# First MLP products by Strassen's scheme, with stored weight operands and unsplit attention

## The chip, the core and the metric

The kernel runs on one core of a Trainium2 chip. The metric is the device time of one execution in microseconds. Before the change three runs gave 1202.59, 1205.68 and 1206.07 us, median 1205.68.

## What is computed

The reference is a retention layer, then two MLPs. All tensors of activations are float32; the weights arrive as 8-byte floats. Cut to what matters:

```python
# q, k, v: (4, 8, 768, 64);  gamma = 1 - 2**(-5 - head)
for t in range(768):
    state = gamma * state + outer(k[:, :, t], v[:, :, t])
    y[:, :, t] = (1 / 8) * q[:, :, t] @ state
x = y.transpose(0, 2, 1, 3).reshape(3072, 512)
h = x @ w_in                      # (512, 2048)
x = np.maximum(0.01 * h, h) @ w_out
h = np.maximum(x @ w_in2, 0)
out = (h * h) @ w_out2            # (3072, 512)
```

## The kernel before

The sequence is cut into three chunks of 256 tokens; a pair is one chunk of one batch entry (`u` in the code) and two heads. For a pair the kernel makes scaled queries `qs` and values `vs`, the masked scores `pm`, the values product `y` and, but for the last chunk, the state that the next chunk starts from (`outer`, `sp`). Pairs with `u` under `WHOLE` (the first chunk) use full float32 matmuls. Later ones split every operand into a high part and a remainder in the `F32R` type (`kh`, `kl`, `q2`, `v2`, `ph`, `w2`) and add up partial products of these.

The MLPs run over six blocks of 512 tokens per layer and, in a block, over 16 steps, one per 128 hidden columns. A step makes the first product (`emit_in`, L407: 4 row blocks x 3 passes = 12 matmuls of 512 columns into one PSUM tile `h`), the activation (`activate`), the split of `g` into `gh` and `gl` (L431, L432), and the second product (`emit_out`, L467: 3 passes x 4 = 12 matmuls into the four `acc` tiles). A product of split operands takes three passes: high by high, remainder by high, high by remainder. Weights are turned from 8-byte to 4-byte floats once, by `cast` (L307 to L313), and stay in SBUF; their split into high part and remainder (`split_w`, L369 and L370) is made anew for every step of every block. For the first `HS` steps of the first block full float32 matmuls of 256 columns are used.

The order on each engine is set by a scheduler that runs when the kernel is built and moves instructions by its own estimate of times; on the chip each engine then runs its list in that order. SP issues the loads and the stores, in its own order. The main loop places attention pairs beside the steps by `place`; four pairs come ahead of the first step.

Names used below: a unit of TensorE's work is one matmul of 512 columns; L numbers are lines of the kernel before unless the kernel after is named.

## Time and profile before

| | |
|---|---|
| three runs | 1202.59, 1205.68, 1206.07 us |
| span of the profiled execution | 1203.3 us; no other time of that execution is given |
| mean granted TensorE clock | 0.995 of 2.4 GHz |
| DMA traffic | 68.80 MB, 57 GB/s in the mean |
| DMA of SP's queue | 67.12 MB, 16.6% of the 16 engines' span |

The profile is of one execution. A page gives busy times by engine, the chain of work that ended last, and groups of instructions by line; the trace behind it can be asked for timelines and tables of stretches. PE is TensorE, DVE VectorE, ACT ScalarE, SP the engine that issues most DMAs. Matmuls overlap and their ends are modelled, so the distance between two starts, not the duration shown, tells the rate; some matmul records can be missing. A busy time is an average over stages with different bounds.

### The profile page before, as it was taken

What the parts mean: (1) busy time and instruction counts of PE and PEld (TensorE: products, weight loads), DVE (VectorE), ACT (ScalarE), POOL (GpSimd) and SP (SyncE); (2) the same over time, 40 slices, a digit from 0 to 9 for tenths busy, and PEclk for the clock granted to TensorE, in tenths of its full rate; (3) what the DMA queues carried; (4) which work ended last, traced back from release to release, by engine and by line L of the source; (5) the groups of instructions that cost most, each with busy time, mean ns of one, the idle gap of its engine ahead of it and who ended that gap; (6) DMA issues with size and microseconds to landing.
All of it is one profiled execution on the core that took longest, in us unless ns stands there. A gap on an engine that the chain in (4) does not pass through costs nothing.

```text
span 1203.3 us, 15155 instructions
## 1 busy us (share of the span) xinstructions
PE 1180.2 (98%) x5670; PEld 976.2 (81%) x5670; DVE 862.4 (72%) x1572; ACT 692.8 (58%) x1352; POOL 0.2 (0%) x4
## 2 busy tenths in 40 slices
PE   7799999999999999999999999999999999999998
PEld 4577788888888888888888788888888888888886
DVE  5898698888889888887888964645555545545553
ACT  4775576666667667676676654544444444444443
POOL 0000000000000000000000000000000000000000
PEclk8999999999999999999999999999999999999999
DMA  9753111111111111110144300000000000000000
GB/s 338 259 205 123 54 44 44 49 44 62 44 40 36 53 36 35 51 38 18 53 149 148 114 28 1 35 1 1 36 1 1 36 1 1 35 1 1 36 1 35
DMA packets 22824, 68.80 MB, mean 57 GB/s; under 512 B 2784, under 2 KB 5088, under 8 KB 22752
## 3 DMA queue, kind: packets, MB, share of 16 engines
q1 hardware_dynamic: 22032, 67.12, 16.6%
q8 instruction: 44, 0.72, 0.2%
q10 hardware_dynamic: 720, 0.73, 0.2%
q14 instruction: 28, 0.23, 0.1%
HBM read 61.55 MB, written 6.29 MB: 56 GB/s over the span
## 4 chain that ended last, share of the span: by engine, by line
PE 89%; DMA 4%; DVE 4%; ACT 2%; issue 1%; DVEq 0%; SPq 0%; ACTq 0%
PE acc L467 40%; PE h L407 40%; DMA sg<-w 4%; PE sc L179 2%; PE y L211 2%; PE sp L246 1%; ACT w L307 1%; PE y L231 1%; DVE w L313 1%; DVE w L310 1%; PE y L205 1%; PE sc L171 1%; PE sc L170 1%; ACT sg L308 0%; DVE w L309 0%
## 5 line engine op out<-in xcount | busy, mean ns | idle before, releaser
L407 PE MATMUL h<-xh,wih 128*128 128x512 f32 (+1 forms) x768 | 298.9, 390 | 1.1 <-DVE g L422 1.1
L407 PE MATMUL h<-xh,wil 128*128 128x512 f32 (+1 forms) x768 | 297.6, 387 | 0.8 <-DVE wil L370 0.8
L407 PE MATMUL h<-xl,wih 128*128 128x512 f32 (+1 forms) x768 | 297.6, 388 | 0.0
L370 DVE TENSOR_TENSOR wol<-w,woh 128x512 fp32r<-128x512 f32 x192 | 132.5, 690 | 150.6 <-ACT woh L369 149.2
L369 ACT CAST woh<-w 128x512 fp32r<-128x512 f32 x192 | 119.5, 622 | 183.5 <-PE acc L467 182.4
L407 PEld LDWEIGHTS h<-xh,wil 128*128 128x128 f32 x768 | 144.2, 188 | 30.3 <-DVE wil L370 1.6
L407 PEld LDWEIGHTS h<-xh,wih 128*128 128x128 f32 x768 | 144.3, 188 | 29.2 <-DVE g L422 1.3
L407 PEld LDWEIGHTS h<-xl,wih 128*128 128x128 f32 x768 | 144.2, 188 | 29.0 <-DVE w L313 0.3
L431 ACT CAST gh<-g 128x512 fp32r<-128x512 f32 (+1 forms) x192 | 118.1, 615 | 38.2 <-DVE g L425 26.4
L432 DVE TENSOR_TENSOR gl<-g,gh 128x512 fp32r<-128x512 f32 (+1 forms) x192 | 130.7, 681 | 11.4 <-ACT gh L431 3.2
L370 DVE TENSOR_TENSOR wil<-w,wih 128x512 fp32r<-128x512 f32 x192 | 131.2, 684 | 0.6 <-ACT wih L369 0.2
L369 ACT CAST wih<-w 128x512 fp32r<-128x512 f32 x192 | 117.5, 613 | 4.7 <-PE h L407 4.4
L467 PE MATMUL acc<-gh,woh 128*128 128x512 f32 (+1 forms) x388 | 111.7, 396 | 0.5 <-ACT gh L431 0.5
L425 DVE SCALAR_TENSOR_TENSOR g<-h,g 128x512 f32<-128x512 f32 x96 | 66.3, 690 | 62.9 <-ACT g L424 62.8
L467 PE MATMUL acc<-gh,wol 128*128 128x512 f32 (+1 forms) x388 | 108.9, 385 | 0.0
L467 PE MATMUL acc<-woh,gh 128*128 128x512 f32 x384 | 108.5, 389 | 0.0
L467 PE MATMUL acc<-wol,gh 128*128 128x512 f32 x384 | 108.5, 389 | 0.0
L467 PE MATMUL acc<-woh,gl 128*128 128x512 f32 x384 | 107.0, 389 | 0.0
L467 PE MATMUL acc<-gl,woh 128*128 128x512 f32 (+1 forms) x388 | 103.9, 384 | 0.0
L424 ACT ACTIVATE g<-h 128x512 f32<-128x512 f32 x96 | 57.3, 597 | 77.3 <-PE h L407 73.5
L421 ACT ACTIVATE g<-h 128x512 f32<-128x512 f32 (+1 forms) x101 | 57.9, 573 | 50.1 <-PE h L407 40.5
L467 PEld LDWEIGHTS acc<-woh,gh 128*128 128x128 f32 x384 | 72.1, 188 | 15.0
(84 smaller groups left out, 1453.8 us busy)
## 6 DMA issues: line engine op xcount, KB each, us to landing
sg<-w SPq DMA_DIRECT2D x64, 512.0 KB, 3.8
r<-attn SPq DMA_DIRECT2D x32, 512.0 KB, 3.5
out<-os SPq DMA_DIRECT2D x24, 256.0 KB, 2.2
re<-first SPq DMA_DIRECT2D x9, 512.0 KB, 5.6
r<-first SPq DMA_DIRECT2D x6, 512.0 KB, 3.9
kn<-attn SPq DMA_DIRECT2D x16, 128.0 KB, 2.0
r<-first SPq DMA_DIRECT2D x2, 256.0 KB, 3.2
qt<-qtab ACTq DMA_DIRECT2D x1, 384.0 KB, 7.8
```

The lines of the kernel that those rows point to most:

```text
L170: nc.tensor.matmul(out=sc[:, 128:256], lhsT=k[a, P:2 * P], rhs=qs[a, P:2 * P], start=True, stop=True)
L179: nc.tensor.matmul(out=sc[:, o:o + C - c], lhsT=kk[:, h * C + sb * P:h * C + (sb + 1) * P], rhs=q2[h][:, c:C], start=n == 0 and sb == 0, s ...
L211: nc.tensor.matmul(out=y[:, c:C], lhsT=v2[:, sb, h].rearrange("p a e -> p (a e)"), rhs=t[:, n, o:o + C - c], start=start, stop=n == 1 and ...
L369: nc.scalar.copy(hi, src)
L370: nc.vector.tensor_tensor(out=lo, in0=src, in1=hi.bitcast(F32), op=ALU.subtract)
L407: nc.tensor.matmul(out=hp[:, :c1 - c0], lhsT=a[:, kb * P:(kb + 1) * P], rhs=b[:, c0:c1], start=kb == 0 and k == 0, stop=kb == KB - 1 and k ...
L421: nc.scalar.activation(out=g[:, :m], in_=hp[:, :m], func=AF.Copy, scale=LEAK)
L424: nc.scalar.activation(out=g[:, :m], in_=hp[:, :m], func=AF.Relu)
L425: nc.vector.scalar_tensor_tensor(out=g[:, :m], in0=hp[:, :m], scalar=0.0, in1=g[:, :m], op0=ALU.max, op1=ALU.mult)
L431: nc.scalar.copy(gh[:, :m], g[:, :m])
L432: nc.vector.tensor_tensor(out=gl[:, :m], in0=g[:, :m], in1=gh[:, :m].bitcast(F32), op=ALU.subtract)
L467: nc.tensor.matmul(out=o, lhsT=lhsT, rhs=rhs, start=start and k == 0, stop=stop and k == 2)
```

## The change

The token blocks of both MLPs become 1024 wide, three per layer. For each group `q` of 256 hidden columns, the first product of a 512 x 256 weight with a 512 x 1024 activation is taken as a product of 2 x 2 blocks and made with seven block products in place of eight (Winograd's form of Strassen's scheme). Each block product has a contraction of 256, so two row blocks x three passes = 6 matmuls of 512 columns. The sums of weight blocks are made in `make_in`, those of activation blocks in `operands`, and those of products partly in PSUM (tile `pa` carries products 1, 6, 7 and 4 in turn and is copied in between) and partly on VectorE. The second product is as before, once for the first 512 tokens beside the group (`emit_out(lay, b, 0, ...)`, a block's first half here) and once for the other 512 after all groups (`emit_out(lay, b, 1, ...)`, its second half).

The weight operands, high part and remainder, are made once per layer, in its first block or, for four groups of the second layer, in the last block of the first layer. They are stored to DRAM by POOL's queue and read back by SP for every later block, the second product's (`wo`, 1 MB per group) twice per block. Buffers: two for `wo`; one for `wa` and `wb`, the first product's operands, until the attention is done, and two after that. The first layer's output goes through DRAM (`ydr`).

Attention is unsplit in all chunks, the scores of two heads next to each other, and the carried state is a block-diagonal 128 x 128 operand `sdiag`. All 16 pairs of the first chunk come ahead of the MLPs. Scores of later chunks use the same three PSUM tiles as the products. The leaky gate is one VectorE operation on SBUF after a plain copy, where it was a scaled ScalarE copy and a maximum. The output is written in another layout and put in order when it is returned.

Over the program the order of the kernel after holds 2016 matmuls of the first products (its L322) and 2304 of the second (L394), and SP's holds 80 loads of `wo`, 36 each of `wa` and `wb`, 47 + 2 of pairs, 32 of raw weights of 1 MB, 3 of `xs` and 48 stores; POOL's has 48 stores of weight operands.

```diff
+UNIT = {7: 0, 4: 1, 2: 2, 1: 3, 5: 4, 6: 5, 3: 6}
...
+    def swap_pools():
+        early.close()
+        late["p"] = ctx.enter_context(tc.tile_pool(name="late", bufs=1))
...
+    def scores(up):
+        qs, k, vs = prep[up]
+        k0 = 2 * (ups.index(up) % 2)
+        if up[0] < B:
+            sc = [ps_acc.tile([P, 512], F32, tag=f"acc{k0 + h}", name="sc") for h in range(2)]
+        else:
+            sc = [ps_h.tile([P, 512], F32, tag="h", name="sc") for h in range(2)]
...
+                ins = nc.tensor.matmul(out=sc[h][:, cols], lhsT=k[a, kk], rhs=qs[a, qq], start=True, stop=True)
+                if n:
+                    tc.keep_in_program_order(ins)
...
+        y = ps_a.tile([P, 2, C], F32, tag="y", name="y")
+        if c:
+            nc.tensor.matmul(out=y[:, 0], lhsT=sdiag[:, b, p], rhs=qs, start=True, stop=False)
...
+    def attend(n):
+        while n_prep[0] < min(n, len(ups)):
+            up = ups[n_prep[0]]
+            n_prep[0] += 1
+            loads_to(n_prep[0])
+            prep_pair(up)
+            scores(up)
+            loads_to(n_prep[0] + 1)
+            values(up)
...
+    def in_tiles(lay, q):
+        pool = late["p"] if late and q % 2 else w_p
+        a = pool.tile([P, 2, 4, 256], F32R, tag="wa", name="wa", bufs=1)
+        c = pool.tile([P, 2, 3, 256], F32R, tag="wb", name="wb", bufs=1)
+        return a, c
...
+    def make_in(lay, q, ahead=False):
+        load_w(lay, q, 0)
+        f = w_p.tile([P, 7, 256], F32, tag="wf", name="wf", bufs=1)
+        cast(stage.pop((lay, q, 0)), f[:, 1:5].rearrange("p n c -> p (n c)"))
+        nc.vector.tensor_tensor(out=f[:, 0], in0=f[:, 3], in1=f[:, 4], op=ALU.subtract)
+        nc.vector.tensor_tensor(out=f[:, 4], in0=f[:, 4], in1=f[:, 1], op=ALU.add)
+        nc.vector.tensor_tensor(out=f[:, 5], in0=f[:, 1], in1=f[:, 0], op=ALU.subtract)
+        nc.vector.tensor_tensor(out=f[:, 6], in0=f[:, 2], in1=f[:, 5], op=ALU.subtract)
+        if ahead:
+            a = late["p"].tile([P, 2, 4, 256], F32R, tag="ea", name="ea")
+            c = late["p"].tile([P, 2, 3, 256], F32R, tag="eb", name="eb")
+        else:
+            a, c = in_tiles(lay, q)
+        for t, s in ((a, f[:, 3:7]), (c, f[:, 0:3])):
+            nc.scalar.copy(t[:, 0], s)
+            nc.vector.tensor_tensor(out=t[:, 1], in0=s, in1=t[:, 0].bitcast(F32), op=ALU.subtract)
+        nc.gpsimd.dma_start(out=wid[lay, q][:, 0:2048], in_=a.rearrange("p l n c -> p (l n c)").bitcast(F32))
+        nc.gpsimd.dma_start(out=wid[lay, q][:, 2048:3584], in_=c.rearrange("p l n c -> p (l n c)").bitcast(F32))
+        if not ahead:
+            put_in(lay, q, a, c)
+
+    def read_in(lay, q):
+        a, c = in_tiles(lay, q)
+        nc.sync.dma_start(out=a.rearrange("p l n c -> p (l n c)").bitcast(F32), in_=wid[lay, q][:, 0:2048])
+        nc.sync.dma_start(out=c.rearrange("p l n c -> p (l n c)").bitcast(F32), in_=wid[lay, q][:, 2048:3584])
+        put_in(lay, q, a, c)
+
+    def get_in(lay, b, q):
+        (make_in if b == 0 and q >= lay * NQ // 2 else read_in)(lay, q)
+
+    def make_out(lay, q):
+        load_w(lay, q, 1)
+        f = w_p.tile([P, 1024], F32, tag="wf", name="of", bufs=1)
+        cast(stage.pop((lay, q, 1)), f)
+        o = w_p.tile([P, 2, 2, 512], F32R, tag="wo", name="wo", bufs=2)
+        fv = f.rearrange("p (j c) -> p j c", j=2)
+        nc.scalar.copy(o[:, 0], fv)
+        nc.vector.tensor_tensor(out=o[:, 1], in0=fv, in1=o[:, 0].bitcast(F32), op=ALU.subtract)
+        nc.gpsimd.dma_start(out=wod[lay, q], in_=o.rearrange("p l j c -> p (l j c)").bitcast(F32))
+        wout[lay, q] = o
+
+    def read_out(lay, q):
+        o = w_p.tile([P, 2, 2, 512], F32R, tag="wo", name="wo", bufs=2)
+        nc.sync.dma_start(out=o.rearrange("p l j c -> p (l j c)").bitcast(F32), in_=wod[lay, q])
+        wout[lay, q] = o
...
+    def operands(lay, b):
+        if lay == 1:
+            xs[NB + b] = x_p.tile([P, KB, TB], F32, tag="xs", name="xs")
+            nc.sync.dma_start(out=xs[NB + b], in_=ydr[b])
+        x = xs.pop(lay * NB + b)
+        b11, b12, b21, b22 = x[:, 0:2, 0:T], x[:, 0:2, T:TB], x[:, 2:4, 0:T], x[:, 2:4, T:TB]
+        o = {}
+        tt = nc.vector.tensor_tensor
+        o[1] = split(1, b11)
+        tt(out=b11, in0=b12, in1=b11, op=ALU.subtract)
+        o[5] = split(5, b11)
+        o[3] = split(3, b22)
+        tt(out=b12, in0=b22, in1=b12, op=ALU.subtract)
+        tt(out=b22, in0=b22, in1=b11, op=ALU.subtract)
+        o[6] = split(6, b22)
+        o[7] = split(7, b12)
+        o[2] = split(2, b21)
+        tt(out=b21, in0=b21, in1=b22, op=ALU.subtract)
+        o[4] = split(4, b21)
+        xop[lay, b] = o
...
+    def product(lay, b, q, i, ps, first_mm, last_mm):
+        w, x = win[lay, q][i], xop[lay, b][i]
+        for kt in range(2):
+            c = slice(kt * P, kt * P + P)
+            for k, (l, r) in enumerate(((0, 0), (1, 0), (0, 1))):
+                nc.tensor.matmul(
+                    out=ps, lhsT=w[l][:, c], rhs=x[r][:, kt], start=first_mm and kt == 0 and k == 0,
+                    stop=last_mm and kt == 1 and k == 2, skip_group_check=True,
+                )
...
+    def act_sbuf(lay, g, on_act):
+            nc.vector.scalar_tensor_tensor(out=g, in0=g, scalar=0.01, in1=g, op0=ALU.mult, op1=ALU.max)
...
+    def emit_in(lay, b, q):
+        j0, j1 = 2 * q, 2 * q + 1
+        pa = ps_h.tile([P, T], F32, tag="h", name="pa")
+        product(lay, b, q, 1, pa, True, True)
+        c11 = g0[j0] = keep(pa, "g", 3)
+        pd = ps_h.tile([P, T], F32, tag="h", name="pd")
+        product(lay, b, q, 5, pd, True, True)
+        c22 = g1[j1] = keep(pd, f"t{j1}", 1)
+        product(lay, b, q, 6, pa, False, True)
+        c12 = g1[j0] = keep(pa, f"t{j0}", 1)
+        product(lay, b, q, 3, pd, False, True)
+        nc.vector.tensor_tensor(out=c12, in0=c12, in1=pd, op=ALU.add)
+        act_sbuf(lay, c12, True)
+        product(lay, b, q, 7, pa, False, True)
+        nc.vector.tensor_tensor(out=c22, in0=c22, in1=pa, op=ALU.add)
+        act_sbuf(lay, c22, True)
+        pb = ps_h.tile([P, T], F32, tag="h", name="pb")
+        product(lay, b, q, 2, pb, True, True)
+        nc.vector.tensor_tensor(out=c11, in0=c11, in1=pb, op=ALU.add)
+        act_sbuf(lay, c11, False)
+        product(lay, b, q, 4, pa, False, True)
+        g = g0[j1] = g_p.tile([P, T], F32, tag="g", name="g", bufs=3)
+        if lay == 0:
+            nc.scalar.copy(g, pa)
+            act_sbuf(lay, g, False)
...
-    def split_w(i, half):
...
-        nc.scalar.copy(hi, src)
-        nc.vector.tensor_tensor(out=lo, in0=src, in1=hi.bitcast(F32), op=ALU.subtract)
...
+    attend(B * NP)
+    make_in(0, 0)
+    operands(0, 0)
+    make_out(0, 0)
+
+    for lay in range(2):
+        for b in range(NB):
+            fresh = b == 0
+            nxt = (b + 1) * B * NP if lay == 0 else 0
+            start_at = n_prep[0]
+            for q in range(NQ):
+                emit_in(lay, b, q)
+                if q + 1 < NQ:
+                    get_in(lay, b, q + 1)
+                if lay == 0 and b == NB - 1 and q % 2:
+                    make_in(1, q // 2, True)
+                if lay == 0 and b + 1 < NB:
+                    per = 1 if fresh else 2
+                    attend(start_at + per * (q + 1))
+                gg = [split_g(g0.pop(j)) for j in (2 * q, 2 * q + 1)]
+                for n, j in enumerate((2 * q, 2 * q + 1)):
+                    emit_out(lay, b, 0, j, gg[n])
+                if q + 1 < NQ:
+                    (make_out if fresh else read_out)(lay, q + 1)
+                else:
+                    read_out(lay, 0)
+            evacuate(lay, b, 0)
+            last = lay == 1 and b == NB - 1
+            if not last:
+                nl, nb = (lay, b + 1) if b + 1 < NB else (1, 0)
+            for j in range(NJ):
+                gg = split_g(g1.pop(j))
+                emit_out(lay, b, 1, j, gg)
+                if j % 2 == 1 and j + 1 < NJ:
+                    read_out(lay, j // 2 + 1)
+                if lay == 0 and b + 1 < NB and j < 8:
+                    attend(min(start_at + B * NP, n_prep[0] + 1))
+                if not last and j == 9:
+                    operands(nl, nb)
+                    get_in(nl, nb, 0)
+            if not last:
+                (make_out if nb == 0 else read_out)(nl, 0)
+            evacuate(lay, b, 1)
+            if (lay, b) == (0, NB - 2):
+                swap_pools()
```

On VectorE in the first layer, one step of the kernel before in the stage with attention (`wol`, `wil` remainders of the weights, `gl` that of the activation, the others attention and the gate):

```order
L370 TENSOR_TENSOR wol<-w,woh 128x512
L189 TENSOR_TENSOR pm<-sc,mk 128x384
L422 TENSOR_TENSOR g<-g,h 128x512
L259 TENSOR_TENSOR t<-state,sp 64x64 x2
L370 TENSOR_TENSOR wil<-w,wih 128x512
L138 TENSOR_TENSOR kl<-r,kh 128x512
L260 TENSOR_SCALAR state<-t,gt 128x64
L195 TENSOR_TENSOR ph<-pm,ph 128x384
L432 TENSOR_TENSOR gl<-g,gh 128x512
```

In the kernel after, part of one group of the first block, on VectorE (`wf`, `wa`, `wb`: the next group's weights; `pd`, `pa`: PSUM tiles of products; L334 is the gate):

```order
L352 TENSOR_TENSOR g<-g,pd 128x512
L216 TENSOR_SCALAR wf<-wf 128x1024
L334 SCALAR_TENSOR_TENSOR g<-g 128x512
L355 TENSOR_TENSOR g<-g,pa 128x512
L217 SCALAR_TENSOR_TENSOR wf<-sg,wf 128x1024
L334 SCALAR_TENSOR_TENSOR g<-g 128x512
L220 ISA wf<-sg,wf 128x2048
L133 TENSOR_TENSOR pm<-sc,mk 128x384 x2
L106 TENSOR_TENSOR qs<-r,qt 128x256
L239 TENSOR_TENSOR wf<-wf 128x256
L169 SCALAR_TENSOR_TENSOR sdiag<-sp,gt,scar 64x64 x2
L334 SCALAR_TENSOR_TENSOR g<-g 128x512
```

The remainders of weights that stood in every step are gone; conversions and sums of the next group's weights stand between the sums of this group's products, in one queue.

On TensorE in the second layer, before (`h` is a first product, `acc` the second):

```order
L407 MATMUL h<-xl_9813,wih 128x512
L407 MATMUL h<-xh_9814,wih 128x512
L407 MATMUL h<-xh_9814,wil 128x512
L467 MATMUL acc<-woh,gh 128x512 x4
L467 MATMUL acc<-wol,gh 128x512 x4
L467 MATMUL acc<-woh,gl 128x512 x4
L407 MATMUL h<-xl_9815,wih 128x512
```

and after, in the second half of a block of the second layer, where the products (`pd`, `pa`) are those of the next block:

```order
L394 MATMUL acc<-gh,wo 128x512 x8
L394 MATMUL acc<-gl,wo 128x512 x4
L394 MATMUL acc<-gh,wo 128x512 x8
L394 MATMUL acc<-gl,wo 128x512 x4
L322 MATMUL pd<-xh_7397,wa 128x512 x2
L322 MATMUL pd<-xl_7398,wa 128x512
L322 MATMUL pd<-xh_7397,wa 128x512 x2
L322 MATMUL pd<-xl_7398,wa 128x512
L394 MATMUL acc<-gh,wo 128x512 x8
L394 MATMUL acc<-gl,wo 128x512 x4
```

Both kinds of product still alternate; each run of 24 `acc` matmuls uses one `wo` tile that SP has read from DRAM.

## Rows read from the trace of the kernel before

**Rows 1.** Page, first part: busy us of each engine, share, instructions.
```profile
PE 1180.2 (98%) x5670; PEld 976.2 (81%) x5670; DVE 862.4 (72%) x1572; ACT 692.8 (58%) x1352; POOL 0.2 (0%) x4
```

**Rows 2.** Table of stretches: us; busy us (instructions) by engine; PEclk, DMA share, GB/s.
```profile
0.00:30.00 30.00, 21.63 (x107) 14.79 (x107) 17.46 (x33) 13.11 (x25) 0.20 (x4) 0.83 0.91 338
30.00:61.00 31.00, 23.66 (x136) 17.67 (x136) 27.54 (x40) 23.97 (x37) 0.00 (x0) 1.00 0.73 264
...
821.00:908.00 87.00, 87.00 (x386) 72.06 (x385) 46.89 (x72) 39.75 (x68) 0.00 (x0) 1.00 0.04 13
```

**Rows 3.** Chain of waits, second layer: start us, us, what.
```profile
848.07 4.08 PE h L407 x18
...
1109.19 4.08 PE h L407 x18
```

**Rows 4.** Timeline of TensorE, two steps with one split pair: start us, us, what.
```profile
306.32 1.17 PE L467 MATMUL acc<-gh,woh 128*128 128x512 f32 x4
...
319.82 1.17 PE L467 MATMUL acc<-gh,woh 128*128 128x512 f32 x4
```

**Rows 5.** Timeline of TensorE, unsplit pairs of the first chunk and their neighbours.
```profile
47.24 1.89 PE L397 MATMUL h<-xs,w 128*128 128x256 f32 x8
49.06 0.87 PE L231 MATMUL y<-pm,vs 128*64 128x256 f32 x8
49.86 0.50 PE L170 MATMUL sc<-qs,r 64*128 64x128 f32 x4
50.19 0.61 PE L171 MATMUL sc<-qs,r 64*128 64x256 f32 x4
...
64.22 0.49 PE L170 MATMUL sc<-qs,r 64*128 64x128 f32 x2
...
65.07 0.50 PE L407 MATMUL h<-xh,wil 128*128 128x512 f32 x1
...
93.83 0.71 PE L246 MATMUL sp<-vs,r 128*128 128x128 f32 x4
94.30 1.17 PE L467 MATMUL acc<-gh,woh 128*128 128x512 f32 x4
```

**Rows 6.** Groups by line and shape: count | busy us, mean ns of one | idle before.
```profile
L370 DVE TENSOR_TENSOR wol<-w,woh 128x512 fp32r<-128x512 f32 x192 | 132.5, 690 | 150.6 <-ACT woh L369 149.2
...
L424 ACT ACTIVATE g<-h 128x512 f32<-128x512 f32 x96 | 57.3, 597 | 77.3 <-PE h L407 73.5 <-DVE gl L432 3.6
...
L189 DVE TENSOR_TENSOR pm<-sc,mk 128x384 f32<-128x384 f32 x96 | 53.0, 555 | 24.9 <-PE sc L179 17.8 <-PE sc L171 6.1
...
L310 DVE SCALAR_TENSOR_TENSOR w<-sg,w 128x1024 uint32<-128x1024 uint32 x16 | 19.5, 1221 | 0.2
...
L313 DVE CUSTOM_DVE_ANT_0 w<-sg,w 128x2048 uint16<-128x2048 uint16 x16 | 19.5, 1221 | 1.0 <-ACT w L307 0.5
...
L123 DVE TENSOR_TENSOR qs<-r,qt 128x256 f32<-128x256 f32 x39 | 16.5, 423 | 23.6 <-DMA r<-attn 23.6
...
L309 DVE TENSOR_SCALAR w<-w 128x1024 uint32<-128x1024 uint32 x16 | 11.0, 688 | 2.2 <-ACT w L307 2.2
...
L259 DVE TENSOR_TENSOR t<-state,sp 64x64 f32<-64x64 f32 x32 | 6.9, 216 | 0.3
```

**Rows 7.** Timeline of the start: VectorE's first work on loaded data.
```profile
4.84 0.42 DVE L124 TENSOR_TENSOR vs<-r,vt 128x256 f32<-128x256 f32 x1 [3.45 <-DMA r<-first]
```

**Rows 8.** DMA issues: count, KB each, median us to landing; whole span, then 0 to 30 us.
```profile
sg<-w SPq DMA_DIRECT2D x64, 512.0 KB, 3.8
...
out<-os SPq DMA_DIRECT2D x24, 256.0 KB, 2.2
...
GB/s 0 0 124 282 315 292 260 290 329 381 410 399 434 414 421 410 421 426 399 396 391 395 392 404 426 410 399 415 410 399 421 426 344 180 104 339 273 169 388 426
...
sg<-w SPq DMA_DIRECT2D x13, 512.0 KB, 6.9
```

**Rows 9.** Timeline of the end: TensorE's last matmuls.
```profile
1197.20 1.07 PE L467 MATMUL acc<-woh,gl 128*128 128x512 f32 x4
```

More of the change, by code (lines that the diff above doesn't have):

```diff
@@ L150, in prep_pair @@
-        if chunk(u):
-            s = state[:, u % B, p]
-            w2 = st_p.tile([P, 2, 2, D], F32R, tag="w2", name="w2")
+        prep[up] = (qs, t[:, C:2 * C], vs)
+    def scores(up):
[5 more added lines that the diff above has]
+            sc = [ps_h.tile([P, 512], F32, tag="h", name="sc") for h in range(2)]
+        n = 0
+        for cols, kk, qq in ((slice(128, 256), slice(P, 2 * P), slice(P, 2 * P)), (slice(256, 512), slice(0, P), slice(0, C))):
@@ L278, in retention_then_two_mlps @@
-    wraw, stage = {}, {}
-    tiles = [(lay, j) for lay in range(2) for j in range(NJ)]
-    n_loaded, n_conv = [0], [0]
-    def load_tile():
-        m = n_loaded[0]
-        if m < len(tiles):
-            lay, j = tiles[m]
-            if lay == 0:
-                t = slot((4, 5, 3)[j % 3], [P, 2, DM], U64, "sg")
-                stage[m] = [t[:, 0], t[:, 1], t]
-            else:
-                stage[m] = [stage_p.tile([P, DM], U64, tag="sg", name="sg") for half in range(2)]
-            for half in range(2):
-                nc.sync.dma_start(out=stage[m][half], in_=w[lay, j, half])
-            n_loaded[0] += 1
@@ L305, in cast, with load_w @@
+    for b in range(NB):
+        ydr[b] = dram.tile([P, KB, TB], F32, name=f"ydr{b}")
+    src = (w1, w2)
+    stage = {}
+    def load_w(lay, q, half):
+        t = stage[lay, q, half] = w_p.tile([P, 1024], U64, tag="sg", name="sg", bufs=2)
+        nc.sync.dma_start(out=t, in_=src[lay][q, half])
+    def cast(s, r):
+        word = s.bitcast(U32).rearrange("p (n t) -> p n t", t=2)
         lo, hi = word[:, :, 0], word[:, :, 1]
@@ L321, in convert @@
+    def act_sbuf(lay, g, on_act):
         if lay == 0:
-            cast(got[2].rearrange("p h n -> p (h n)"), r)
-        else:
-            for half in range(2):
-                cast(got[half], r[:, half * DM:(half + 1) * DM])
-        if n_loaded[0] < NJ or lay == 1:
-            load_tile()
-    def converted_to(n):
-        while n_conv[0] < min(n, len(tiles)):
-            back = n_conv[0] - BEHIND
-            if 0 <= back and n_conv[0] < NJ:
-                with tc.issue_after(gate[back].ins):
-                    convert()
-            else:
-                convert()
@@ new lines, in retention_then_two_mlps, with split_g, emit_out @@
+    acc = {}
+    def split_g(g):
+        gh = g_p.tile([P, T], F32R, tag="gh", name="gh")
+        gl = g_p.tile([P, T], F32R, tag="gl", name="gl")
+        nc.scalar.copy(gh, g)
+        nc.vector.tensor_tensor(out=gl, in0=g, in1=gh.bitcast(F32), op=ALU.subtract)
+        return gh, gl
+    def emit_out(lay, b, t, j, gg):
+        if j == 0:
+            acc[lay, b, t] = [ps_acc.tile([P, T], F32, tag=f"acc{m}", name="acc") for m in range(KB)]
+        ac = acc[lay, b, t]
+        o = wout[lay, j // 2]
+        gh, gl = gg
+        passes = ((0, gh), (1, gh), (0, gl))
+        if j in (0, NJ - 1):
+            mm = [(k, m) for m in range(KB) for k in range(3)]
+        else:
+            mm = [(k, m) for k in range(3) for m in range(KB)]
+        for k, m in mm:
+            l, r = passes[k]
+            nc.tensor.matmul(
+                out=ac[m], lhsT=o[:, l, j % 2, m * P:(m + 1) * P], rhs=r,
+                start=j == 0 and k == 0, stop=j == NJ - 1 and k == 2,
+            )
@@ new lines, in evacuate @@
+    def evacuate(lay, b, t):
+        ac = acc.pop((lay, b, t))
+        for m in range(KB):
+            y = g_p.tile([P, T], F32, tag="y", name="y", bufs=2)
+            if m % 2 == 0:
+                nc.scalar.copy(y, ac[m])
+            else:
+                nc.vector.tensor_copy(y, ac[m])
+            dst = ydr[b] if lay == 0 else out[b]
+            nc.sync.dma_start(out=dst[:, m, t * T:(t + 1) * T], in_=y)
+    nc.gpsimd.memset(sdiag, 0.0)
+    zero = g_p.tile([P, T], F32R, tag="gh", name="zero")
```

578 lines of the change are left out of this document (132 added, 446 removed).

## The prediction

> **What bounds the kernel now.** I read the page's first part, then a table of stretches, then the chain of waits in the second layer, then timelines of the places that the change touches. TensorE is busy 98% of the span, VectorE 72% [rows 1]. In a stretch of the second layer TensorE is busy in 87.00 of 87.00 us while VectorE works 46.89 [rows 2]: nothing but matmul time counts there. At the start it is otherwise: in the first 30 us TensorE is busy 21.63 us at a granted clock of 0.83, in the next 31 us 23.66 us, and the reader is to see that VectorE fills 27.54 of those 31 [rows 2].
>
> In the second layer one 512-token block begins at 848.07 and the one three later at 1109.19 [rows 3]: 87.04 us for 16 x (12 + 12) = 384 matmuls of 512 columns, 226.7 ns each. That is my unit.
>
> **The MLP matmuls.** A 1024-token block of one layer had 2 x 384 = 768 units. Now a group of two hidden blocks takes 7 products x 2 x 3 = 42 in place of 48, eight groups 336, and the second product keeps 384: 720 units, 163.2 us. Over six blocks 4608 units become 4320: 288 x 0.2267 = 65.3 us less. TensorE is the bound, so all of it counts wherever VectorE and the loads keep up.
>
> **Attention.** Two steps of 24 units with one split pair between them take 319.82 - 306.32 = 13.50 us [rows 4]; less 48 units (10.88), a split pair costs 2.62 us; without the state product (0.47, the distance 93.83 to 94.30 [rows 5]) 2.15. An unsplit pair: the scores of one head alone take 65.07 - 64.22 = 0.85, of both heads side by side 49.86 to 50.80, 0.94 with the drain of the last, so 0.85 again; values 49.86 - 49.06 = 0.80; state product 0.47; and the carried state as a full fp32 matmul of 256 columns 1.82 / 4 = 0.455 (four from 47.24 to 49.06) [rows 5]. That is 2.12 in the first chunk, 2.58 in the second, 2.11 in the third. Between other matmuls a pair pays for the changeover; I add 0.2 (bounds: 0, and 0.85 if the heads don't run side by side), so 2.78 and 2.3 against 2.62 and 2.15. Over 16 pairs each this is 5 us worse. The casts that it spares ScalarE and VectorE lay beside TensorE and are worth nothing by themselves.
>
> **Where VectorE becomes the bound.** All 16 pairs of the first chunk now come ahead of the MLPs, with the first weights and the first operands of the products. Up to the first result c11, VectorE runs 34 query and value scalings of 0.42, 32 masks of 0.555, three conversions of 1024 columns (0.688 + 1.221 + 1.221), eight sums of 256 columns at 0.42, weight remainders for 3.4 (0.95 for 768 columns, between 0.69 for 512 and 1.22 for 1024), four operand steps of 1.22 and two of 0.69 [rows 6]: 54.2 us. The first data is used at 4.84 [rows 7]. VectorE was busy (17.46 + 27.54) / (61 - 4.84) = 80% of such a stage before, 89% in its second part, 69% in its first [rows 2]. I take 80%: 4.8 + 67.8 = 72.6 us, with 66 and 83 as bounds. TensorE needs 16 x 2.12 = 33.9 us in it, 68 at half the clock, so it is covered.
>
> Each further group of this block adds on VectorE: weights 2 x (0.688 + 1.221 + 1.221) + 4 x 0.42 + 0.95 + 2 x 1.22 = 11.3; three sums, four gates and two remainders of 512 columns, 9 x 0.69 = 6.2; one pair 2 x 0.42 + 2 x 0.555 + 2 x 0.22 = 2.4. Together 19.9 us [rows 6], while TensorE needs 66 x 0.2267 + 2.78 = 17.7. VectorE ends last, by 2.2 us at least. The operations also wait for TensorE and ScalarE in turn, so I take 21 us a group, between 19.9 (VectorE never idle) and 22.4 (89% busy [rows 2]). The gate costs VectorE 0.69 as before and is within the 6.2; elsewhere it lies beside TensorE. Making the weights is thus paid for once, in this block; in the later ones VectorE has 10 us (6.2 and two pairs' 3.9, or less) in a group of 15 to 20 and is hidden again. In the second layer's first block four groups make both weights: 11.3 + 7 x 0.69 = 16.1 against 15.0 us, about 5 us in all.
>
> **The loads.** The made weights are written once and read back: 80 tiles of 1 MB and 36 of 1.8 MB read, 46 MB stored, 34 of raw weights, 23 of pairs, 19 of activations: 272 MB against 68.8. Over 1175 us that is 231 GB/s; in the first 30 us the engines moved around 400 GB/s in most of 40 slices [rows 8]. The bandwidth is there; the question is latency. In a block's second half a 1 MB tile serves 24 matmuls, 5.44 us, and two buffers take turns, so it has 5.44 us from issue to landing. The trace has no 1 MB load. A 512 KB one lands in 3.8 us (median) and in 6.9 in the crowded first 30 us; 256 KB out takes 2.2 [rows 8]. So 1 MB lies between 3.8 and 7.6 (two after one another). I take 5.1, the 3.8 of the first half and 1.3 for 512 KB more at 400 GB/s: no wait when alone. Products of the next block stand between those matmuls and give room. I put 10 us on waits for loads and hand-overs, bounds 0 and 104 (2.16 us x 8 tiles x 6 blocks).
> The Trainium skill, "DMA: Bandwidth & Descriptors", section "Anatomy of one DMA — SWDGE (gpsimd) path", fits a transfer as 2.0 us plus its bytes at 436 GB/s, for the gpsimd path. By it 512 KB would land in 3.2 us, which the trace shows slower, and 1 MB in an estimated 4.4; the sum would then lose the 10 us and stand at 1167. No load of that size was run.
>
> **The sum**, against the profiled execution: 72.6 to the first c11; seven groups 147; the rest of that half, 58 units and a pair, 15.9; its second half 192 units and eight pairs of 2.78, 65.7; five blocks at 163.2, 816; sixteen pairs at 2.3, 36.8; second-layer weights 5; waits 10; from the last matmul to the end 1203.3 - 1198.1 = 5.2 as before [rows 9]. 1174 us against the span of 1203.3. The three runs have a median of 1205.7, 2.4 above that span, so 1177.
>
> **Rivals.** (1) The loads decide, slower than before. Place: the second half of every block, where the next tile is issued when the one before last is released, and what stands behind it in SP's queue waits too. If 1 MB lands in 7.6 us, TensorE waits 2.16 us on each of 48 tiles: 1167 + 104 = 1271. It beats the gain from 0.8 us a tile on (38 / 48), a landing of 6.2. For it: 512 KB took 6.9 us when the engines were crowded. Against it: the mean load is near half of what they have moved, and matmuls of the next block lie between.
> (2) Hand-overs. One PSUM tile now carries products 1, 6, 7 and 4 in turn and is copied in between, and the scores use the same three tiles. If each of 7 x 48 products waits 0.15 us, a quarter of one 0.6 us copy [rows 6], this costs 50 us in place of the 10: 1217. For it: the engines run a fixed order made for other durations. Against it: TensorE waited nowhere in the second layer with the same kind of order.
> (3) VectorE's order in the first block is close to gapless and the start as good as its second part: 66 + 7 x 19.9 and no waits: 1177 - 6.6 - 7.7 - 15 = 1148.
> (4) That the matmuls are not saved: they are, by the count of rows in the order, 2016 in the first products in place of 2304.
>
> **Chances.** Forecast 0.52 (own range 1158 to 1200), (1) 0.15, (2) 0.15, (3) 0.18. The range runs from 1138, (3) with pairs that pay no changeover (32 x 0.2) and a little beside, to 1230, which takes in (2) and (1) up to six tenths of its price. A difference of under 0.3% (3.6 us) can't be told from none. Faster: the forecast 0.51, (3) 0.18, a third of (2), 0.05: 0.74. Same: 0.05 out of (1), (2) and the forecast. Slower: 0.21.
>
> **What would show it.** Right: TensorE's share near 85% up to some 300 us and near full after it; VectorE without gaps between about 70 and 220 us; units 227 ns apart in the second layer; blocks of about 163 us there. The step on the loads is wrong if TensorE's idle time names reads of the stored weights; that on hand-overs if it names ScalarE's copies in the second layer; that on VectorE if its busy share up to 220 us is under 80%. A steady block of 174 us, twice the 87.04 of before, would have given the saved matmuls back and make the prediction wrong.

## The result, and the profile after

The changed kernel takes 1220.5 us (median of four runs, 1212.8 to 1228.4) against 1205.1 of the kernel before: ratio 1.0127, 95% interval 1.0085 to 1.0169. It is slower by 1.3%, where 1177 was forecast. The profiled execution has a span of 1216.9 us, 42.9 over the 1174 of the sum.

The page's first part, to be held against [rows 1]:
```profile
PE 1143.3 (94%) x5290; PEld 897.3 (74%) x5290; DVE 670.6 (55%) x1003; ACT 487.3 (40%) x771; POOL 27.7 (2%) x53
```
TensorE has 37 us less work and VectorE 192 us less, and yet the span is 13.6 us longer: TensorE now stands idle for 74 us, where it was 23. The table of stretches (us; busy us by engine; PEclk, DMA share, GB/s) shows where:
```profile
0.00:30.00 30.00, 19.76 (x84) 13.34 (x85) 17.01 (x29) 14.89 (x28) 3.20 (x7) 0.68 0.81 294
30.00:61.00 31.00, 20.30 (x144) 12.80 (x142) 20.25 (x41) 15.38 (x42) 0.53 (x1) 0.86 0.59 211
80.30:237.90 157.60, 140.28 (x636) 103.25 (x634) 133.95 (x198) 79.21 (x102) 10.64 (x20) 0.99 0.61 229
345.70:445.20 99.50, 99.50 (x512) 74.70 (x511) 46.69 (x86) 21.66 (x40) 0.00 (x0) 1.00 0.54 186
714.00:832.00 118.00, 108.40 (x455) 86.44 (x454) 99.84 (x125) 79.83 (x109) 7.98 (x15) 0.97 0.70 261
942.10:972.00 29.90, 29.90 (x134) 24.76 (x133) 9.46 (x15) 11.81 (x21) 0.00 (x0) 1.00 0.51 194
1157.60:1217.00 59.40, 46.85 (x194) 37.63 (x192) 13.02 (x19) 11.09 (x19) 0.00 (x0) 0.91 0.46 159
```
Of the 74 us, 65 lie at the start (25 up to 80.3 us), in the first layer's first block (third row), in the second layer's first block (fifth) and at the end (last). In the fourth and sixth rows TensorE has no gap. VectorE, 27.54 us busy of 31 in the second stretch of [rows 2], is now 20.25 there. The granted clock (PEclk) is 0.68 and 0.86 of 2.4 GHz in the first two rows, where it was 0.83 and 1.00.

VectorE's sum that completes c11 comes once a group, so its starts mark the groups (start us, us, line, operands; releaser of the idle time in brackets):
```profile
80.32 0.69 DVE L359 TENSOR_TENSOR g<-g,pb 128x512 f32<-128x512 f32 x1 [0.30 <-PE pb L322]
...
237.89 0.69 DVE L359 TENSOR_TENSOR g<-g,pb 128x512 f32<-128x512 f32 x1
...
942.11 0.68 DVE L359 TENSOR_TENSOR g<-g,pb 128x512 f32<-128x512 f32 x1
957.07 0.68 DVE L359 TENSOR_TENSOR g<-g,pb 128x512 f32<-128x512 f32 x1
```
The first comes at 80.3 us and the eighth 157.6 later, 22.5 us a group. In the second layer the distance is 14.96, which is 66 units of 226.7 ns, the unit of [rows 3]: the matmuls are saved, and where nothing else is in the way their time is too.

### The profile page after: what moved, and what is told of

Read it like the earlier page. It is cut to its first block, busy times and chain, and to the rows that moved or that the text cites. A ratio compares the mean times of both kernels' runs of the same rounds, so it can differ in the third digit from the quotient of the medians.

```text
span 1216.9 us, 13751 instructions
## 1 busy us (share of the span) xinstructions
PE 1143.3 (94%) x5290; PEld 897.3 (74%) x5290; DVE 670.6 (55%) x1003; ACT 487.3 (40%) x771; POOL 27.7 (2%) x53
## 4 chain that ended last, share of the span: by engine, by line
PE 80%; DMA 9%; DVE 7%; ACT 3%; issue 1%; SPq 0%; ACTq 0%; DVEq 0%
PE acc L394 40%; PE pa L322 19%; PE pd L322 10%; PE pb L322 5%; PE sc L126 3%; DMA r<-first 2%; PE y L148 2%; DMA sg<-w 2%; DMA out<-y 2%; DVE xl L289 1%; PE y L144 1%; DVE wf L220 1%; DMA mk<-mask 1%; DMA ydr<-y 1%; DMA wo<-wod 1%
## 5 line engine op out<-in xcount | busy, mean ns | idle before, releaser
L394 PE MATMUL acc<-gh,wo 128*128 128x512 f32 x1536 | 399.8, 396 | 13.8 <-ACT y L404 8.2
L394 PEld LDWEIGHTS acc<-gh,wo 128*128 128x128 f32 x1536 | 287.7, 189 | 83.8 <-ACT y L404 11.4
L378 DVE TENSOR_TENSOR gl<-g,gh 128x512 fp32r<-128x512 f32 x192 | 131.8, 689 | 182.3 <-PE acc L394 151.6
L394 PE MATMUL acc<-gl,wo 128*128 128x512 f32 x768 | 217.3, 393 | 0.0
L377 ACT CAST gh<-g 128x512 fp32r<-128x512 f32 x192 | 118.7, 621 | 236.0 <-PE acc L394 177.8
L394 PEld LDWEIGHTS acc<-gl,wo 128*128 128x128 f32 x768 | 144.1, 189 | 31.5 <-issue 1.4
L322 PE MATMUL pa<-xh,wa 128*128 128x512 f32 x384 | 124.4, 400 | 15.2 <-ACT wa L249 9.1
L322 PE MATMUL pa<-xh,wb 128*128 128x512 f32 x384 | 121.1, 396 | 4.1 <-DVE g L355 2.7
L322 PE MATMUL pd<-xh,wa 128*128 128x512 f32 x384 | 121.9, 393 | 0.6 <-ACT g L329 0.6
L322 PEld LDWEIGHTS pa<-xh,wa 128*128 128x128 f32 x384 | 71.5, 189 | 37.5 <-ACT wa L249 11.7
L329 ACT COPY g<-pa 128x512 f32<-128x512 f32 x96 | 56.3, 586 | 93.4 <-PE pa L322 87.6
L322 PEld LDWEIGHTS pa<-xh,wb 128*128 128x128 f32 x384 | 71.2, 188 | 22.0 <-DVE g L355 4.4
L334 DVE SCALAR_TENSOR_TENSOR g<-g 128x512 f32<-128x512 f32 x96 | 66.1, 689 | 32.2 <-ACT g L364 30.9
L322 PEld LDWEIGHTS pd<-xh,wa 128*128 128x128 f32 x384 | 71.8, 188 | 16.4 <-ACT g L329 1.7
L322 PE MATMUL pa<-xl,wa 128*128 128x512 f32 x192 | 75.5, 393 | 1.2 <-DVE xl L289 1.2
L322 PE MATMUL pd<-xl,wa 128*128 128x512 f32 x192 | 74.9, 390 | 0.5 <-DVE xl L289 0.5
L322 PE MATMUL pa<-xl,wb 128*128 128x512 f32 x192 | 74.8, 390 | 0.0
L352 DVE TENSOR_TENSOR g<-g,pd 128x512 f32<-128x512 f32 x48 | 33.0, 687 | 65.3 <-PE pd L322 41.1
L359 DVE TENSOR_TENSOR g<-g,pb 128x512 f32<-128x512 f32 x48 | 32.9, 686 | 53.6 <-PE pb L322 49.3
L322 PE MATMUL pb<-xh,wb 128*128 128x512 f32 x192 | 61.9, 398 | 0.5 <-ACT g L364 0.5
L329 ACT COPY g<-pd 128x512 f32<-128x512 f32 x48 | 28.2, 588 | 72.6 <-PE pd L322 68.5
```

Source lines behind the costliest of these rows:

```text
L322: nc.tensor.matmul(out=ps, lhsT=w[l][:, c], rhs=x[r][:, kt], start=first_mm and kt == 0 and k == 0, stop=last_mm and kt == 1 and k == 2, s ...
L329: nc.scalar.copy(t, ps)
L334: nc.vector.scalar_tensor_tensor(out=g, in0=g, scalar=0.01, in1=g, op0=ALU.mult, op1=ALU.max)
L352: nc.vector.tensor_tensor(out=c12, in0=c12, in1=pd, op=ALU.add)
L359: nc.vector.tensor_tensor(out=c11, in0=c11, in1=pb, op=ALU.add)
L377: nc.scalar.copy(gh, g)
```

## Experiments

Each kernel is timed against the kernel before on the same chip; "ratio" is to that one. Lines of code in headings are those of the changed kernel, lines in rows those of the kernel shown. "Off" is a difference of medians to the changed kernel's 1220.5 us, whose own interval is 5 us wide to either side; where a gain is of that size, the stage in the trace has to bear it out. The order on each engine is made anew with every edit, so an edit can move more than it names.

**1. The change without Strassen's scheme.**
```
-  seven products of 6 matmuls (i = 1, 5, 6, 3, 7, 2, 4), seven operand splits,
-  four sums of weights, four of operands, three of results
+  for t, p: ps = A[p,0] B[0,t] + A[p,1] B[1,t]   (8 x 6 matmuls, four operand splits, no sums)
```


> The first product without Strassen's scheme: eight quarter products in place of seven, on the same 1024-token blocks, with weight tiles still made once and reread from DRAM (1 MB in place of 1.8 MB), four operand splits in place of seven and no sums of weights, operands or products on VectorE. 768 units of 0.2267 us a block in place of 720. Theory A (the saved matmuls are real, but the work that the scheme puts on VectorE in the first block, with the start, gives them back): the five later blocks take 10.9 us more each, 54; in the first block a group needs 15.2 us of VectorE and 18.9 of TensorE, so it takes about 19.5 in place of 22.5 and the first half loses 21 us; the start shortens by the three operand steps and the four sums, 5 to 8 us; the second layer's first block gains about 10 of its 15 lost us; total about 1232, so the scheme is worth some 15 us of its 65. Rival B (rereading and the 1024-token blocks cost what was lost, the scheme itself costs nothing): 1217 + 65 = 1282, with groups still near 22 us. Rival C (unsplit attention lost it): like B.

Measured: 1229.9 us, ratio 1.0205 (1.0190 to 1.0221); theory A. The scheme is worth 9.4 us where TensorE saves 65.3; in the profiled executions it is 10.6 (1227.5 against 1216.9 us), so 54.7 are given back. The first copies out of four half blocks (ScalarE) show where, this kernel first, then the changed kernel:
```profile
234.15 0.59 ACT L364 COPY y<-acc 128x512 f32<-128x512 f32 x1 [0.41 <-PE acc L354]
716.52 0.59 ACT L364 COPY y<-acc 128x512 f32<-128x512 f32 x1 [1.19 <-PE acc L354]
890.99 0.58 ACT L364 COPY y<-acc 128x512 f32<-128x512 f32 x1
1173.94 0.59 ACT L364 COPY y<-acc 128x512 f32<-128x512 f32 x1 [0.91 <-PE acc L354]
```
```profile
253.92 0.59 ACT L404 COPY y<-acc 128x512 f32<-128x512 f32 x1
714.41 0.59 ACT L404 COPY y<-acc 128x512 f32<-128x512 f32 x1
894.23 0.58 ACT L404 COPY y<-acc 128x512 f32<-128x512 f32 x1
1157.63 0.58 ACT L404 COPY y<-acc 128x512 f32<-128x512 f32 x1
```
By the first row the kernel with the scheme is 19.8 us late although it has 48 units (10.9 us) fewer to do: 30.7 given back. From the second to the third row it needs 179.8 us against 174.5, where it has 10.9 fewer: 16.2. From the last to the span's end it needs 59.3 against 53.6: 5.7. That is 52.6 of the 54.7. Of the 30.7 only 1.6 lie ahead of the first product (it starts at 74.9 us against 73.3; 5 to 8 were expected), so 29 lie in the eight groups. The 5.7 at the end are not work of the scheme's own; experiment 3 shows what they are.

**2. Raw attention pairs ahead** (changed kernel L91 to L98).
```
-  t = a_p.tile([P, FW], F32, tag="r", name="r")            # two in turn
+  t0, t1 = two [P, T] tiles out of t4 to t15, for the first 22 pairs
-  loads_to(n_prep[0] + 1)
+  loads_to(n_prep[0] + 4)                                  # up to pair 18
```


> The raw tiles of the first 22 attention pairs lie in twelve 256 KB tiles that stand empty until the later groups (six pairs at once in place of two), and are asked for up to four pairs ahead. Nothing else is changed. Theory A1 (in the start VectorE stands still for raw pairs because two buffers let only two loads be under way: 3.45 us a pair from 36 us on, where a pair's own work is near 2.1): the first c11 comes at about 66 us in place of 80, the groups of the first block lose the 4.8 us that VectorE waited for raw pairs in 80 to 238 us; total 15 to 19 us less, about 1200. Rival A2 (VectorE's own work and the hand-overs between the engines set the start, as the prediction had it; the loads only look late): the first c11 at 77 to 83 us, total within 4 us of before this edit. Rival A3 (the DMA engines themselves are full there, 0.81 busy in the first 30 us): loads asked for earlier land later, gain 3 to 6 us, nearly all after 30 us.

Measured: 1205.1 us, ratio 0.9995 (0.9985 to 1.0005), so 15 us off; A1. VectorE in the changed kernel, then here:
```profile
52.67 0.43 DVE L107 TENSOR_TENSOR vs<-r,vt 128x256 f32<-128x256 f32 x1 [1.90 <-DMA r<-first]
...
59.53 0.42 DVE L107 TENSOR_TENSOR vs<-r,vt 128x256 f32<-128x256 f32 x1 [1.91 <-DMA r<-first]
```
```profile
53.89 0.42 DVE L111 TENSOR_TENSOR vs<-r,vt 128x256 f32<-128x256 f32 x1 [0.72 <-PE y L152]
...
56.81 0.42 DVE L111 TENSOR_TENSOR vs<-r,vt 128x256 f32<-128x256 f32 x1 [0.72 <-PE y L152]
```
Two pairs took 6.9 us and waited for a load; now one takes 2.9 and TensorE releases it. The first c11 comes at 66.6 us. VectorE does the same work up to it, 47.7 us from 4.5 us on (47.9 from 4.8 on before), and is 77% busy in place of 63%. The prediction's lower bound of 66 rested on 54.2 us of work at 89%; that it is met is chance. The seven groups still take 156.4: the 4.8 us of waits for raw pairs in them were not what set them (VectorE's wait for ScalarE's weight step grows from 8.8 to 11.1 instead), and that part of A1 is wrong.

**3. Tiles of their own for the last results** (L402).
```
-  y = g_p.tile([P, T], F32, tag="y", name="y", bufs=2)
+  y = ye[:, m, t * T:(t + 1) * T] if last block else (as before)   # ye: the free operand buffer
```


> The last block's eight result tiles get places of their own (in the operand buffer that is free by then) in place of two tiles that take turns. Theory: the 8 us between the copies of 1157.6 and 1165.9 are waits for stores of 5.7 us that hold the two tiles; TensorE loses 5.5 us there and the end after the last matmul shortens from 7.6 to near 5: total 7 to 8 us less. Rival (the stores are at their rate there, and the last of them ends as late as before): 0 to 2 us less.

Measured: 1212.5 us, ratio 1.0071 (1.0049 to 1.0093): 8 us off; the theory. The interval just overlaps the changed kernel's, but in the profiled executions the stretch from the last block's first copy to the end falls from 59.3 to 51.8 us. The rows from the changed kernel that say why:
```profile
1165.87 0.59 ACT L404 COPY y<-acc 128x512 f32<-128x512 f32 x1 [7.67 <-DMA out<-y]
1166.48 0.69 DVE L406 COPY y<-acc 128x512 f32<-128x512 f32 x1 [7.64 <-DMA out<-y]
1166.51 0.79 PE L394 MATMUL acc<-gh,wo 128*128 128x512 f32 x1 [5.24 <-ACT y L404]
```
The third and fourth accumulators wait 7.7 us for a store to give back one of two tiles, and the matmuls of the second half need those accumulators: TensorE stands for 5.2 us. Earlier in the program such waits cost it 2.7 us in all; there it has products of the next block to do, and behind the last block there are none. The gap costs more than its length, because the granted clock behind it is 0.52 of 2.4 GHz, near the lower of its two levels, 1.2 GHz:
```profile
1166.50:1171.80 5.30, 5.29 (x13) 4.19 (x14) 1.37 (x2) 0.81 (x2) 0.00 (x0) 0.52 0.26 99
```
Its 12 matmuls between 1166.51 and 1171.71 us start 0.43 apart in place of 0.2267, some 2.5 us lost.

Two tiles alone do not make this wait. Experiment 1 has the same two and loses nothing; its stores go out ahead of a 1 MB read of `wo`, those of the changed kernel behind it (experiment 1 first):
```profile
1174.55 1.12 SPq L368 DMA_DIRECT2D out<-y  x2
1175.97 0.33 SPq L263 DMA_DIRECT2D wo<-wod  x1
1176.66 0.59 ACT L364 COPY y<-acc 128x512 f32<-128x512 f32 x1 [0.29 <-DMA out<-y]
```
```profile
1158.00 0.32 SPq L278 DMA_DIRECT2D wo<-wod  x1
1158.37 0.90 SPq L408 DMA_DIRECT2D out<-y  x2
```
The tile is back 2.1 us after its store was issued there and 7.5 us here. That the read ahead of it is the reason was not tested.

**4. Weight conversion without VectorE's three steps** (L216 to L220).
```
-  nc.vector.tensor_scalar(... logical_shift_left)
-  nc.vector.scalar_tensor_tensor(... bitwise_and, bitwise_or)
-  nc.vector.tensor_tensor(... add)                         # ScalarE's two steps stay and swap places
```


> Leaves out the three VectorE steps of each weight conversion (0.69 + 1.22 + 1.22 us, 32 times), so the weights' values are wrong; ScalarE's two steps, the sums, the splits and all loads and stores stay. Theory A (VectorE's order is what makes a group of the first block 22.5 us in place of TensorE's 17.7): VectorE has 6.3 us less to do in a group, groups come to 18 to 19 us, first half 25 to 30 us less; start 3 to 6 us less; second layer's first block 8 to 12 us less; total 36 to 48 less, about 1175. Rival (waits on loads and ScalarE's copies set the group, VectorE only follows): groups 21 us or more, total less than 15 us less.

Measured: 1187.6 us, ratio 0.9857 (0.9833 to 0.9881), 33 us off, a little under the 36 to 48 expected; theory A. Groups of the first block, and the second layer's first half block:
```profile
82.50:218.50 136.00, 132.10 (x624) 101.03 (x625) 97.93 (x160) 77.16 (x102) 10.63 (x20) 1.00 0.70 266
700.00:803.00 103.00, 103.00 (x455) 85.16 (x454) 69.48 (x93) 78.67 (x110) 7.97 (x15) 1.00 0.84 310
```
Seven groups fall from 157.6 to 136.0, VectorE's busy share from 85 to 72%, TensorE's rises from 89 to 97%; the second layer's 118 become 103, without a gap. The start did not get shorter (first c11 at 82.6, where 3 to 6 us less were expected), which fits experiment 2: loads set it. The edit shortens the chain of weight steps along with VectorE's work; experiment 5 tells the two apart.

**5. The leaky gate on ScalarE** (L334, L364).
```
-  nc.vector.scalar_tensor_tensor(out=g, in0=g, scalar=0.01, in1=g, op0=ALU.mult, op1=ALU.max)
+  nc.scalar.activation(out=g, in_=g, func=AF.Lrelu, alpha=0.01)
```


> The first layer's leaky gate goes from VectorE to ScalarE's own leaky function: in place after the sum for three results of a group, straight from PSUM (in place of copy and gate) for the fourth. VectorE has 4 x 0.69 = 2.8 us less to do in a group, ScalarE 3 x 0.6 = 1.8 us more; the making of the weights, its buffers and its order of steps stay. Theory A-sum (the amount of VectorE's work sets the first block's groups): 19.1 - 2.8 = 16.3 us of VectorE, so groups of 22.5 fall to 19.5 to 20.5, seven of them 14 to 21 us less; total about 1202. Theory A-chain (the latency of the chain of weight steps, ScalarE to VectorE and back in one staging buffer, sets them; leaving out the three conversion steps shortened that chain too): groups stay at 22 to 22.5, total within 4 us of before this edit. Nothing is expected in blocks 1 and 2, where VectorE lies beside TensorE.

Measured: 1211.9 us, ratio 1.0044 (1.0024 to 1.0065), 8.6 us off. Groups:
```profile
79.30:221.60 142.30, 134.47 (x633) 102.64 (x632) 118.86 (x170) 87.31 (x122) 10.64 (x20) 1.00 0.66 253
```
15.3 us less in seven groups, with nothing changed in the chain of weight steps: A-sum. VectorE's share is 84%, as it was 85%. Of the 15.3 us 11.6 arrive at the end of the profiled execution (1205.3 against 1216.9). Part is lost in the second half of the next block, where TensorE waits 4.8 us for one tile of the second product's weights while the DMA engines are 0.94 busy (465 to 541 us); the changed kernel waits 2.4 us there.

**6. All of the second layer's weights made a block earlier.**
```
-  if lay == 0 and b == NB - 1 and q % 2: make_in(1, q // 2, True)
+  if lay == 0 and b == NB - 1: make_in(1, q, True)     # and make_out(1, j // 2, True) in the second half
```


> All sixteen weight tiles of the second layer are made and stored during the first layer's last block (four were before), and its first block rereads them like the others. Theory A: the 15 us that TensorE lost between 714 and 833 us were VectorE's making of twelve tiles; they go, the last block of the first layer takes 16 x 5.6 = 90 us more or less beside TensorE's 163 (VectorE had 73 of 165 us in use with four of them), and the total falls 11 to 15 us, to about 1204. Rival A-move: twelve more made tiles make the last block of layer one wait as the other did, gain under 5 us. Rival (the second layer's first block loses its time to hand-overs or loads, not to making): gain under 3 us.

Measured: 1217.8 us, ratio 1.0091 (1.0067 to 1.0115): 4.3 us by the ratios, which the two intervals cannot tell from nothing. The first layer's last block and the second layer's first half block:
```profile
554.00:730.00 176.00, 169.29 (x730) 137.00 (x729) 125.09 (x162) 87.61 (x122) 8.50 (x16) 0.99 0.92 350
730.00:833.00 103.00, 102.55 (x452) 84.43 (x452) 46.07 (x62) 46.50 (x75) 0.00 (x0) 1.00 0.58 206
```
The 118 us became 103, as with the conversion left out, and the block before grew from 165 us (549 to 714) to 176 and began 5 us later; the profiled spans are the same, 1216.8 and 1216.9. The loss moved with the making, as A-move had it, here beside DMA engines that are 0.92 busy.

**7 to 9. Together, and the scheme once more.** Experiment 7 is edits 2, 3, 5 and 6; 8 is 2, 3 and 5; 9 is 8 without the scheme.

> Raw pairs ahead, end tiles, gate on ScalarE and the second layer's weights ahead, all four together. If the four losses are separate (start, groups of the first block, second layer's first block, end): 1217 - 15 - 8 - 17 - 13 = about 1164. If raw pairs ahead and the gate overlap (both shorten the same groups): up to 1172. If VectorE's amount does not set the groups: about 1181.

> Raw pairs ahead, end tiles and the gate on ScalarE, without the second layer's weights ahead. If the three losses add up: 1220 - 15 - 8 - 8 = 1189, some 2 to 5 us above the kernel that also made the second layer's weights ahead. If that fourth edit costs something once the others are in: 1181 or less.

> The same three edits on the kernel without Strassen's scheme (eight quarter products, four operand splits, no sums). Theory A (most of what the scheme saves on TensorE is given back as VectorE's work in the two first blocks and as waits at start and end, and a kernel in which these are smaller keeps more of it): from 1230 the raw pairs take off 13, the end tiles 0 to 3 (it lost nothing between 1174 and 1220), the gate 3 to 8: about 1210, so the scheme is worth 20 to 30 us beside the kernel with it, in place of 10 to 13. Rival (the edits help both alike): 1198 to 1202, the scheme still worth 10 to 13.

Measured: 7: 1183.7 us, ratio 0.9815 (0.9798 to 0.9832); 8: 1188.2, 0.9854 (0.9838 to 0.9871); 9: 1214.1, 1.0062 (1.0047 to 1.0077). Three losses add up (1189 expected in 8). I expected 1164 to 1172 of 7 because I took 17 us for the gate and 13 for the weights ahead, before either was measured. In experiment 7 the order changed too: VectorE has 60 us of work ahead of the first c11, which comes at 81.9 us where it is 65.3 in experiment 8, so what each edit gives there can't be told. Experiment 7 is faster than both kernels, by 1.8 and 3.1%. Between 8 and 9 the scheme is worth 25.8 us in place of 9.4: theory A.

**10. The four weight sums on GpSimd.**
```
-  nc.vector.tensor_tensor(out=f[:, 0], in0=f[:, 3], in1=f[:, 4], op=ALU.subtract)   (and three more)
+  nc.gpsimd.tensor_tensor(...)
```


> The three edits, and the four sums of each weight tile (4 x 0.42 us) go from VectorE to GpSimd, which is busy 28 us in all. Theory A-sum: VectorE has 1.7 us less in a group of 16.3, groups fall from 19.3 to 18.6, where TensorE sets them; the second layer's first block loses some 2 to 4 us less; total 5 to 9 us less than with the sums on VectorE. Rival A-chain (each sum on GpSimd takes over twice VectorE's 0.42 us and the weights' chain is longer by 2 us or more a group, or GpSimd's work slows VectorE's): total equal or above.

Measured: 1187.9 us, ratio 0.9844 (0.9829 to 0.9858), the same as experiment 8, as A-chain had it. VectorE's work in seven groups falls by 4.5 us (117.8 to 113.3), not by the 12 of four sums in each, and the groups take 145.2 us against 144.6. So it does not speak against experiment 5. What it shows of the two engines stands in the last section.

## Why the prediction was wrong

Against the profiled execution, term by term (us):

| term | predicted | measured | over |
|---|---|---|---|
| first c11 | 72.6 | 80.3 | 7.7 |
| seven groups | 147 | 157.6 | 10.6 |
| rest of the first half | 15.9 | 16.0 | 0.1 |
| sixteen pairs | 36.8 | 39.5 | 2.7 |
| second layer's weights | 5 | 14.9 | 9.9 |
| end, beside the last 192 units | 5.2 | 15.8 | 10.6 |
| everything else, with the 10 for waits | 891.5 | 892.8 | 1.3 |

The first half block of layer two is 118.0 us for 455 units (103.1); the end is 59.3 us for 192 (43.5).

**The step that failed** is "VectorE ends last, by 2.2 us at least ... so I take 21 us a group, between 19.9 and 22.4", and with it the 5 us for the second layer, which rest on the same work. The amount of work came out near, 133.95 us in seven groups or 19.1 each against 19.9, but by luck: the sum for a group leaves out eight operand steps that fall into these groups (9.8 us), and the single durations that it adds up overlap where instructions follow one another; they come to 145.0 us. And 21 us means a VectorE that is 95% busy, where for the start, a paragraph earlier, I had read 80% from [rows 2]. Measured it is 85% in the groups, and 84% again in experiment 5, with less work. VectorE's two longest waits and TensorE's longest in these groups (us, times, longest) are below; the first and the last lie in the chain of weight steps, which goes back and forth between VectorE and ScalarE, the second is for raw pairs:
```profile
DVE of L216 <- ACT of L214: 8.8, 7, 2.0
DVE vs L107 <- DMA r<-first: 4.8, 6, 2.2
```
```profile
PE pa L322 <- ACT wa L249: 5.8, 4, 2.1
```
The sum had 1.1 us a group for all such waits; they came to 3.4. With the 80 to 89% of [rows 2] the groups would have come out at 22.4 to 24.9 us and the second layer's four at 18 to 20. The mechanism was right and its size was not: experiments 4 and 5 move the groups by taking VectorE work away, and experiments 4 and 6 take the second layer's loss out of its block, 6 by moving it to another.

**The start** was put down to 54.2 us of VectorE's work at 80%. The work was 47.9 us from 4.8 us on, again less than the sum of durations, so at 80% the first c11 would have come at 64.7; the 7.7 us over are the rest of two errors, an amount too high and a share too high (it was 63%). What I left out is that the raw pairs have two buffers, so the load of a pair waits for the state product of the pair two before it, and VectorE for the load (up to 80 us):
```profile
DVE vs L107 <- DMA r<-first: 16.3, 10, 3.4
```
I had counted loads for the steady blocks and not for the start. Experiment 2 takes this away, and VectorE is then 77% busy, near the 80% taken.

**The end** I took over from the kernel before. Its last stores left from four tiles of their own; in the changed kernel eight copies share two, and a 256 KB store takes 5.4 us to land where it took 2.2 [rows 8]. Of the 15.8 us, 5.2 are the gap of experiment 3, some 2.5 the lower clock behind it and 7.6 the time from the last matmul to the end. That two tiles take turns was readable in the code; the landing time under this load, and so the price (experiment 3: 8 us), was in no row.

**What held.** 288 matmuls less at 0.2267 us. Steady blocks at 163 us: groups 14.96 us apart, and two blocks take 325.0 us from the first copy at 832.62 to the one at 1157.63, 162.5 each and not the 174 that would have refuted it. An unsplit pair of the third chunk: 99.5 us for five groups of 66 units and two pairs each, (99.5 - 74.8) / 10 = 2.47 against 2.3 taken and 2.11 to 2.96 as bounds. TensorE near full from 320 us on, except in the two places above. Up to 300 us it was 85% busy, as forecast, though that stage took longer: this sign could not tell the forecast from what happened. The one on VectorE did: its share up to 220 us is 167.25 of 220, 76%, under the 80% that I had named as the sign that the step on VectorE is wrong, and "without gaps" between 70 and 220 us is 125.94 of 150.

**The rivals.** (1) The reads of stored weights do not decide: a 1 MB tile of the second product lands in 4.9 us (5.1 taken), and TensorE waits 2.4 us for such tiles in the whole span. Those of the first product, which were not the rival's, land in 6.7, and TensorE's waits name none of them. The loads that did decide, of raw pairs at the start, were in no rival.
```profile
wo<-wod SPq DMA_DIRECT2D x80, 1024.0 KB, 4.9
wa<-wid SPq DMA_DIRECT2D x36, 1024.0 KB, 6.7
...
wod<-wo POOLq DMA_DIRECT2D x16, 1024.0 KB, 4.9
...
wid<-wa POOLq DMA_DIRECT2D x12, 1024.0 KB, 4.3
...
out<-y SPq DMA_DIRECT2D x24, 256.0 KB, 5.4
wid<-ea POOLq DMA_DIRECT2D x4, 1024.0 KB, 9.4
```
The Trainium skill, "DMA: Bandwidth & Descriptors", section "Anatomy of one DMA — SWDGE (gpsimd) path", fits a transfer on that path as 2.0 us plus its bytes at 436 GB/s, an estimated 4.4 us for 1 MB. The stores on GpSimd's queue took 4.3 and 4.9, so it was near; four took 9.4 in the median, issued between 486 and 540 us, where the DMA engines are 0.97 busy (479 to 549 us). The sum of 1167 that went with it would have been further off. (2) Hand-overs gave 1217, which is the measured span by coincidence: it put its 50 us evenly on 7 x 48 products, and groups in the second layer's steady stretch lose nothing; TensorE's waits for copies of products (L329), the sign that was named, come to 5.8 us in the whole span, 3.7 of them in the second layer's first block. (3) A gapless VectorE is refuted by its 85%. (4) did not happen: 2016 first products.

**Against the kernel before**, 13.6 us in the profiled spans: 65.3 us saved, 79 lost. Without the scheme (experiment 1) 54.7 of the 79 are not lost: 47 in the two blocks where weights are made and 5.7 at the end. Of the other 24, edits 2, 3 and 5 recover 16 in the kernel without the scheme (1230 to 1214), and third-chunk pairs of 2.47 in place of 2.15 account for 5 of the rest by the traces. No run undid the unsplit attention or the 1024-token blocks alone, so how these two share what is left is open.

## What to carry to other kernels

A saving on the engine that bounds a kernel is worth its full size only in the stages where that engine is the bound; price the stages in which the same change makes another engine the bound with that engine's busy share as the trace shows it in such a stage (here 85%), not with 95 or 100%, and with its busy time there, not with single durations added up. Then look at the two ends of the program by themselves, for tiles that take turns: a load into two buffers at the start and a store from two tiles at the end cost 15 and 8 us here, and the steady state showed neither.
